# New orders of issue and new PSUM banks for a linear-attention block with a gated MLP, on one core

## The chip, the core and the metric

The kernel runs on one core of a Trainium2 chip. A core has TensorE (PE, matmuls; its weight loads are shown as PEld), VectorE (DVE), ScalarE (ACT), GpSimd (POOL) and SyncE (SP), which here issues every DMA. TensorE writes its results to PSUM, eight banks; DVE and ACT read them from there. The metric is the device time of one execution in microseconds (us), as the median of several runs.

## The reference

A block of a transformer on 2048 tokens of width 448, in bf16: linear attention with 16 heads of 28, then a gated MLP of width 1792, each behind a layernorm without weights and with a residual.

```python
h  = x + A(layernorm(x))
h2 = h + B(layernorm(h))

# A: phi(t) = where(t > 0, t + 1, exp(t)) + 1e-6
q, k, v = split(x @ wqkv)
kv  = einsum("bhsd,bhse->bhde", phi(k), v);  z = phi(k).sum(tokens)
o   = einsum("bhqd,bhde->bhqe", phi(q), kv) / (einsum("bhqd,bhd->bhq", phi(q), z) + 1e-6)
A   = o @ wo
# B
B   = (gelu(x @ w_gate) * (x @ w_up)) @ w_down
```

All of k and v must be summed over all tokens before the first q can be turned into an output, so the work falls into two halves, with the sum `kv` between them.

## The kernel before

The 2048 tokens are 16 tiles of 128. The Python code does not issue instructions as it goes. It records 942 tasks in a graph (`_Graph.add`), each with its engine, what it reads and what it writes, and numbers them in the order of recording. Two constants then say how they are issued. `ORDERS` holds five strings, one for each of PE, ACT, DVE, POOL and SP; each lists the numbers of that engine's tasks in the order in which the engine issues them. `BANKS` gives a PSUM bank to each of the 218 PSUM tiles. `place` reads both, adds to each PE task that opens a tile the dependences on whoever last wrote or read that bank, and asserts that the five orders do not wait for each other in a circle. `emit` then walks an engine's order and puts before each task the semaphore waits that it needs. Every engine works strictly in its own order: a task that waits holds up all tasks behind it on that engine. The same holds for SP's list of DMA issues.

The tasks by name (the number behind the name is the token tile, for gate/up tasks a running number v):

- Start: `dx` loads tokens, `dwkv`, `dwq`, `dwo`, `dwg`, `dwu`, `dwt`, `dwd` load weights (L342). `warm` (L401) is a burst of 36 matmuls on a tile of ones. POOL's `ones`, `ident`, `eps`, `pqones`, `mones`, `mhalf`, `mask_a` to `mask_d` and `powwarm` fill constants (L365 to L387).
- First layernorm: `ast`, `aag` (DVE statistics, L406 and L407), `anm` (POOL, the negated mean, L411), `aln`, `ars` (ACT, 1/sqrt, L416 and L418), `norm` (DVE for tiles 0 and 1, L439, else POOL, L442). Tiles 0 to 3 are transposed on TensorE (`tr`, L452 to L454) and copied by `ev`; the others by ACT's `dup` (L464) and a DMA transpose `xT` on SP (L470).
- k and v: `kva`, `kvb` (L491 to L499), 4 and 3 pairs of matmuls that use the upper and the lower half of the array's rows at once. `ek` (ACT, exp, L506), `cl` (POOL, clamp, L507), `ph` (DVE, phi(k), L508) and `evv` (ACT, copy of v, L510) empty their PSUM tiles. `acca`, `accb` (L518) add the tile's k'v to the sum in two banks.
- `kz1`, `kz2` (DVE, L534 and L536) take the finished sum out of PSUM.
- q: `qa`, `qb` for two tiles at once (L550), `eq` (ACT, L559), `cq` (POOL, L560), `pq` (DVE, L561), and a DMA transpose `qT` (L563).
- Output of the attention: `nd` (L600, L608), `rd` and `om` (DVE, L617 and L620), a transpose (`tro` and `evo` for the first pair of tiles, L631 and L634, a DMA transpose `oT` for the others, L636), `woa`, `wob` (L652), `hr` (DVE, the residual, L665), and the second layernorm: `bst`, `bag`, then for tiles 0 and 1 `bln`, `brs`, `normh` (L678), `trh` (PE, L685 and L687) and `evh` (L690), for the others POOL's `bve`, `bpw`, `bnm`, `normh` (L697), DVE's `wrap` (L699) and the DMA transpose `hT` (L700).
- MLP: `gua`, `gub` (L769, L772), 4 and 3 pairs of matmuls for each block of the width, for groups of 2, 2, 4, 4 and 4 token tiles; `ge` (ACT, gelu, L795), `hm` (DVE, product, L797). `da`, `db` (L719) are the down projection of two tiles, `down` (L733) that of the last two; `out` (DVE, L739) adds the residual and `dout` (SP, L741) stores the tile.

What decides a wait is thus: where a task stands in its engine's order, and which PSUM tile stood in its bank before. The waits are made here:

```python
for t in self.order["pe"]:
    for tile in t.allocs:
        for b in range(tile.bank, tile.bank + tile.nb):
            old = held.get(b)
            if old is not None:
                for d in [old.alloc[0]] + old.users:
                    self._dep(t, d, tile.alloc[1])
            held[b] = tile
```

Of the kernel before, what the change touches and what calls it, by code (L numbers as in the profile page):

```python
# [14 lines left out]
    "29 35 42 138 50 139 146 147 154 58 155 162 144 163 170 145 152 171 178 153 160 179 186 161 168 187 194 169 176 195 177"  # L15
    " 184 268 202 269 203 210 185 192 211 218 193 200 219 226 201 242 227 243 208 234 209 216 235 250 217 224 251 258 225 232"
    " 259 277 233 240 278 241 248 286 249 256 287 257 264 265 295 361 360 296 313 366 386 387 314 368 369 304 322 305 331 323"
    " 332 381 393 384 394 434 465 435 459 466 460 471 410 472 411 477 507 478 508 441 495 442 496 483 417 489 418 484 490 531"
    " 543 532 537 544 561 538 514 562 515 555 579 556 549 580 550 501 567 723 568 724 502 699 586 700 587 573 730 574 731 621"
    " 609 622 706 610 707 633 603 615 604 634 616 627 657 628 658 639 645 640 646 651 675 669 652 676 663 670 664 681 753 682"  # L20
    " 759 754 747 760 765 748 771 766 777 772 778 783 693 789 694 784 790 813 801 807 814 687 802 808 688 795 849 796 843 825"
    " 844 826 850 867 819 868 820 855 861 856 862 873 897 874 879 898 880 903 885 837 886 904 838 921 891 922 892 909 915 910"
    " 916 831 927 832 928 936 933 939",
    "28 32 33 39 40 47 48 51 55 56 140 65 66 143 151 68 59 78 79 71 148 159 91 81 156 167 84 92 164 175 104 172 94 180 97 183"
    " 105 188 117 118 107 191 130 196 110 123 199 131 273 120 270 207 204 133 212 215 223 220 136 228 244 231 247 239 236 255"
    " 252 263 260 279 282 288 291 300 297 318 315 306 376 309 377 378 324 379 327 333 382 336 458 469 467 463 461 473 475 481"
# [846 lines left out]
```

## Time and profile before

| what | value |
|---|---|
| median of 3 runs | 198.19 us (196.95 to 199.13) |
| span of the profiled execution | 194.1 us |
| its own time | not given apart from the span |
| instructions | 5347 |
| ACT busy | 69.6 us of the span (36%) |
| POOL busy | 48.8 us (25%) |
| HBM | 8.72 MB read, 1.84 MB written |
| granted TensorE clock | 1.000 in the mean |

The span runs from the first to the last instruction of the profiled execution; the time of a run also holds what lies before and after. In a row of a timeline the columns are the start, the duration, engine, line, operation, output and inputs, shapes, the number of instructions that were merged into the row, and in square brackets the idle time before it with what ended it. "SPq" marks the issue of a DMA on SP: its duration is that of the issue, not of the transfer. In the rows of DMA issues the last number is the time from issue to landing. The end of a matmul is modelled, so matmuls that follow each other are drawn overlapping.

### The profile page before, as it was taken

What the parts mean: (1) busy time and instruction counts of PE and PEld (TensorE: products, weight loads), DVE (VectorE), ACT (ScalarE), POOL (GpSimd) and SP (SyncE); (2) the same over time, 40 slices, a digit from 0 to 9 for tenths busy, and PEclk for the clock granted to TensorE, in tenths of its full rate; (3) what the DMA queues carried; (4) which work ended last, traced back from release to release, by engine and by line L of the source; (5) the groups of instructions that cost most, each with busy time, mean ns of one, the idle gap of its engine ahead of it and who ended that gap; (6) DMA issues with size and microseconds to landing.
All of it is one profiled execution on the core that took longest, in us unless ns stands there. A gap on an engine that the chain in (4) does not pass through costs nothing.

```text
span 194.1 us, 5347 instructions
## 1 busy us (share of the span) xinstructions
PE 188.0 (97%) x2183; PEld 108.7 (56%) x2183; DVE 114.6 (59%) x299; ACT 69.6 (36%) x201; POOL 48.8 (25%) x104
## 2 busy tenths in 40 slices
PE   7889999999999999999999999999999999999994
PEld 7336555654598798665444445444455554445563
DVE  4699453599999886668686736424251644244132
ACT  4488867443932243210025343422033432213000
POOL 2379984443605009000037630000000000000000
PEclk9999999999999999999999999999999999999999
DMA  5964645989859996523200320100403000010021
GB/s 148 288 209 94 95 89 128 284 178 195 194 114 193 223 222 178 85 56 70 47 0 3 89 69 0 27 5 0 105 3 118 2 3 0 3 47 0 3 83 59
DMA packets 41209, 18.01 MB, mean 93 GB/s; under 512 B 30177, under 2 KB 41057, under 8 KB 41185
## 3 DMA queue, kind: packets, MB, share of 16 engines
q1 hardware_dynamic: 41184, 17.67, 40.0%
q8 instruction: 17, 0.28, 0.6%
q14 instruction: 8, 0.06, 0.1%
HBM read 8.72 MB, written 1.84 MB: 54 GB/s over the span
## 4 chain that ended last, share of the span: by engine, by line
PE 66%; DMA 3%; DVE 3%; issue 0%; SPq 0%; DVEq 0%
PE ps L769 37%; PE ps L719 19%; PE ps L652 4%; DMA wgu_sb<-in_B_w_up_dram 3%; PE ps L772 3%; PE ps L733 3%; DVE pq L561 1%; PE ps L608 1%; DVE x_sb L665 1%; DVE o L620 0%; SPq L342 0%; DVE st L406 0%; DVE hh L797 0%; DVE x_sb L739 0%; DVE hnT L690 0%
## 5 line engine op out<-in xcount | busy, mean ns | idle before, releaser
L772 PE MATMUL ps<-hnT,wgu_sb 64*128 64x512 bf16 (+1 forms) x490 | 89.1, 333 | 0.2 <-DMA wgu_sb<-in_B_w_up_dram 0.2
L769 PE MATMUL ps<-hnT,wgu_sb 64*128 64x512 bf16 (+1 forms) x490 | 89.1, 333 | 0.0
L795 ACT ACTIVATE gl<-ps 128x256 bf16<-128x256 f32 x112 | 36.0, 384 | 87.4 <-PE ps L772 68.3
L797 DVE TENSOR_TENSOR hh<-ps,gl 128x256 bf16<-128x256 f32 x112 | 41.8, 414 | 39.3 <-ACT gl L795 34.9
L769 PEld LDWEIGHTS ps<-hnT,wgu_sb 64*128 64x128 bf16 x490 | 45.0, 94 | 35.0 <-DVE hh L797 2.3
L772 PEld LDWEIGHTS ps<-hnT,wgu_sb 64*128 64x128 bf16 x490 | 45.0, 94 | 0.6 <-DMA wgu_sb<-in_B_w_up_dram 0.5
L719 PE MATMUL ps<-wd_sb,hh 64*128 64x448 bf16 x392 | 38.9, 349 | 0.0
L719 PEld LDWEIGHTS ps<-wd_sb,hh 64*128 64x128 bf16 x392 | 19.1, 94 | 17.9
L406 DVE BATCH_NORM_STATS2 st<-x_sb 128x6 f32<-128x448 bf16 x32 | 19.2, 612 | 4.5 <-DMA x_sb<-in_A_x_dram 4.5
L739 DVE TENSOR_TENSOR x_sb<-ps,x_sb 128x448 bf16<-128x448 f32 (+1 forms) x17 | 9.8, 589 | 16.6 <-PE ps L719 13.3
L491 PE MATMUL ps<-wkv_sb,xnT 64*128 64x448 bf16 x64 | 14.8, 349 | 0.8 <-DMA xnT<-xn 0.4
L508 DVE SCALAR_TENSOR_TENSOR pk<-ps,tm 128x448 bf16<-128x448 f32 x16 | 9.9, 622 | 8.9 <-POOL tm L507 4.1
L492 PE MATMUL ps<-wkv_sb,xnT 64*128 64x448 bf16 x64 | 14.9, 350 | 0.0
L652 PE MATMUL ps<-wo_sb,oT 64*128 64x448 bf16 x112 | 13.4, 350 | 0.1
L550 PE MATMUL ps<-wq_sb,xnT 64*128 64x448 bf16 x112 | 12.3, 349 | 0.0
L498 PE MATMUL ps<-wkv_sb,xnT 64*128 64x448 bf16 x48 | 11.6, 352 | 0.1
L499 PE MATMUL ps<-wkv_sb,xnT 64*128 64x448 bf16 x48 | 11.6, 352 | 0.0
L665 DVE TENSOR_TENSOR x_sb<-ps,x_sb 128x448 bf16<-128x448 f32 x16 | 9.5, 616 | 2.9 <-PE ps L652 2.8
L559 ACT ACTIVATE e<-ps 128x448 bf16<-128x448 f32 x16 | 8.1, 540 | 7.9 <-PE ps L550 7.9
L560 POOL TENSOR_SCALAR tm<-e 128x448 bf16<-128x448 bf16 x16 | 8.8, 560 | 7.8 <-ACT e L559 6.9
L561 DVE SCALAR_TENSOR_TENSOR pq<-ps,tm 128x448 bf16<-128x448 f32 x16 | 9.5, 612 | 1.9 <-PE ps L492 1.2
L442 POOL TENSOR_SCALAR xn<-x_sb,nm,rs 128x448 bf16<-128x448 bf16 x14 | 10.0, 714 | 1.9 <-ACT rs L418 1.6
(70 smaller groups left out, 163.3 us busy)
## 6 DMA issues: line engine op xcount, KB each, us to landing
out_dram<-x_sb SPq DMA_DIRECT2D x15, 112.0 KB, 1.8
wd_sb<-in_B_w_down_dram SPq DMA_DIRECT2D x3, 448.0 KB, 4.4
wgu_sb<-in_B_w_up_dram SPq DMA_DIRECT2D x3, 384.0 KB, 3.8
wgu_sb<-in_B_w_gate_dram SPq DMA_DIRECT2D x3, 384.0 KB, 5.3
x_sb<-in_A_x_dram SPq DMA_DIRECT2D x2, 448.0 KB, 6.2
wo_sb<-in_A_wo_dram SPq DMA_DIRECT2D x2, 336.0 KB, 5.3
x_sb<-in_A_x_dram SPq DMA_DIRECT2D x4, 112.0 KB, 2.1
wkv_sb<-in_A_wqkv_dram SPq DMA_DIRECT2D x1, 448.0 KB, 3.6
```

The lines of the kernel that those rows point to most:

```text
L406: op("dve", lambda e: e.bn_stats(st[:, t, :], src_ap()), [b_src], [b_st[t]], nm + "st%d" % t, 0.615, key)
L491: e.matmul(ps[:, p_k.bank, 0:D], xnT[A_, k, tok], wkv_sb[A_, k, ck], start=(k == 0), stop=False, skip_group_check=True)
L492: ins = e.matmul(ps[:, p_v.bank, 0:D], xnT[B_, k, tok], wkv_sb[B_, k, cv if k < 3 else ck], start=(k == 0), stop=False, skip_group_check=True)
L498: e.matmul(ps[:, p_k.bank, 0:D], xnT[B_, k, tok], wkv_sb[B_, k, ck], start=False, stop=(k == 2), skip_group_check=True)
L499: ins = e.matmul(ps[:, p_v.bank, 0:D], xnT[A_, k, tok], wkv_sb[A_, k, cv], start=False, stop=(k == 2), skip_group_check=True)
L550: ins = e.matmul(ps[:, p_q[n].bank, 0:D], xnT[rows, k, ts[n] * 128:(ts[n] + 1) * 128], wq_sb[rows, k, :], start=(k == 0 and not second), s ...
L652: ins = e.matmul(ps[:, p_h[n].bank, 0:D], oT2[rows, so, kk, :], wo_sb[rows, kk, :], start=(k == 0 and not second and not res), stop=(secon ...
L719: ins = e.matmul(ps[:, p_d[n].bank, 0:D], hh[rows, j, u * 128:(u + 1) * 128], wd_sb[rows, j, :], start=(j == 0 and not second), stop=(j == ...
L769: e.matmul(ps[:, pa.bank, jj * N:(jj + 1) * N], wgu_sb[A_, wa + k if k < 3 else 3, jc], hnT[A_, k, c0:c0 + N], start=(k == 0 and jj == 0 a ...
L772: ins = e.matmul(ps[:, pb.bank, jj * N:(jj + 1) * N], wgu_sb[B_, wb + k if k < 3 else 3, jc], hnT[B_, k, c0:c0 + N], start=(k == 0 and jj ...
L795: G.add("act", lambda e, gi=gi, cs=cs, p_g=p_g: e.activation(gl[:, gi, cs], ps[:, p_g.bank, cs], AF.Gelu_apprx_tanh), r=[p_g], w=[b_gl[gi] ...
L797: op("dve", lambda e, dst=dst, gi=gi, cs=cs, p_u=p_u, rs_=rs_: e.tensor_tensor(dst, rs_(ps[:, p_u.bank, cs]), rs_(gl[:, gi, cs]), ALU.mult ...
```

## The change

`ORDERS` and `BANKS` are replaced; nothing else in the file differs. Each of the five strings still holds the same task numbers, so each engine issues the same instructions with the same operands except for the PSUM bank, in another order. Of the positions in the orders, 61 of 249 on PE hold the same task as before, 50 of 201 on ACT, 54 of 299 on DVE, 16 of 100 on POOL and 33 of 93 on SP. The new lists come from a search on a timing model in which transfers are late at random.

The core of the diff, the first line of each list (PE, ACT, DVE, POOL, SP) and of the banks:

```diff
@@ -12,45 +12,46 @@
 ORDERS = (
-    "29 35 42 138 50 139 146 147 154 58 155 162 144 163 170 145 152 171 178 153 160 179 186 161 168 187 194 169 176 195 177"
...
+    "29 35 42 138 139 146 50 147 58 154 144 155 162 145 163 152 153 170 160 171 161 178 186 179 187 168 194 169 176 195 177"
...
-    "28 32 33 39 40 47 48 51 55 56 140 65 66 143 151 68 59 78 79 71 148 159 91 81 156 167 84 92 164 175 104 172 94 180 97 183"
...
+    "28 32 39 33 40 47 48 140 55 56 143 65 66 51 148 68 59 78 71 79 151 156 159 81 91 164 84 167 92 172 175 94 104 117 105"
...
-    "30 31 37 18 38 34 44 41 45 20 36 43 52 53 60 62 61 63 75 76 73 74 86 88 89 142 87 127 150 101 99 158 100 102 114 166 112"
...
+    "30 37 44 31 18 38 34 41 36 20 45 43 52 53 60 62 61 63 142 73 75 74 76 88 86 150 87 89 101 158 114 99 100 102 115 166"
...
-    "10 12 11 19 46 49 54 57 64 67 70 141 77 80 149 83 157 90 93 165 96 173 103 116 181 106 189 109 122 197 119 129 274 23"
...
+    "19 23 10 11 12 46 21 24 49 22 54 141 57 64 67 70 149 77 80 157 90 83 165 93 96 103 173 106 181 116 189 109 119 197 122"
...
-    "0 1 2 3 4 5 6 7 8 9 16 13 17 69 72 82 85 15 14 95 98 108 111 124 121 342 134 346 137 345 343 276 344 340 355 285 341 353"
...
+    "0 1 2 3 4 5 6 7 8 9 16 15 17 69 72 82 85 13 14 95 98 352 108 121 111 124 276 134 137 354 346 345 341 349 342 285 343"
...
 BANKS = (
-    "0 1 0 0 2 6 1 2 3 4 0 5 2 4 5 1 4 3 1 0 3 2 1 0 3 2 5 0 1 2 5 3 0 4 1 2 3 4 4 5 5 2 1 4 5 3 6 0 1 2 5 4 3 7 7 6 7 7 3 2"
...
+    "3 6 1 6 4 6 5 3 0 2 5 3 4 1 2 0 5 1 3 4 0 2 5 3 2 0 1 3 4 3 0 5 1 2 3 0 4 1 4 1 2 5 0 3 5 1 1 6 3 2 5 0 3 7 4 6 4 5 4"
```

The same in names, at the places that matter below (before, then after):

```
PE    warm tr0 tr1 kva0 tr2 kvb0 kva1 kvb1 kva2 tr3 kvb2 kva3 acca0 kvb3 kva4 accb0 acca1 kvb4 kva5 accb1 acca2 kvb5 kva6 ...
      warm tr0 tr1 kva0 kvb0 kva1 tr2 kvb1 tr3 kva2 acca0 kvb2 kva3 accb0 kvb3 acca1 accb1 kva4 acca2 kvb4 accb2 kva5 kva6 kvb5 ...
PE    ... qa4 accb13 acca14 qb4 accb14 acca15 accb15 qa6 nd1 nd0 qb6 qa10 tro nda2 ndb2 qb10 woa0 wob0 qa8 qa12 qb8 qa14 qb12 qb14
          trh0 woa2 trh1 wob2 nda6 gua1 ndb6 gua0 ...
      ... qa4 accb12 acca13 qb4 accb13 acca14 accb14 acca15 accb15 qa6 qb6 nd1 nd0 qa10 nda2 qb10 tro ndb2 qa8 woa0 wob0 qb8 qa14 qa12
          qb14 qb12 woa2 wob2 trh0 trh1 nda6 gua1 ndb6 gua0 ...
PE    ... woa6 gua6 wob6 gub6 gua4 woa4 gua5 wob4 gub4 gub5 gua7 gua9 ...
      ... woa6 ndb8 wob6 gua6 gua4 gub6 gub4 woa4 gua5 wob4 gub5 gua8 gua10 ...
PE    ... da10 gub49 gub52 db10 ... da8 da12 db8 db12 down15_0 down14_0 down15_224
      ... da10 gua55 gua53 gua54 gub53 gub54 gub55 db10 da8 da12 db8 db12 down14_0 down15_0 down15_224
ACT   tbl aln0 ars0 aln1 ars1 aln2 ars2 ev2 aln3 ars3 ek0 aln4 ars4 evv0 evv1 dup4 ev3 aln6 ars6 dup5 ek1 ...
      tbl aln0 aln1 ars0 ars1 aln2 ars2 ek0 aln3 ars3 evv0 aln4 ars4 ev2 ek1 dup4 ev3 aln6 dup5 ars6 evv1 ...
DVE   ast0 aag0 ast1 pkones aag1 norm0 ast2 norm1 aag2 ...
      ast0 ast1 ast2 aag0 pkones aag1 norm0 norm1 ev0 v1ones aag2 ...
DVE   ... ph15 pq2 pq3 kz2 kz1 pq4 rd1 rd0 om1 om0 pq5 pq7 evo ... normh0 pq8 pq9 normh1 pq12 pq13 evh1 hr2 hr3 ...
      ... pq3 pq2 ph15 kz1 pq4 kz2 pq5 rd1 rd0 om1 om0 pq7 pq6 evo ... normh0 pq11 normh1 pq12 hr3 evh1 hr2 ...
POOL  ones eps ident pqones anm2 norm2 anm3 norm3 anm4 norm4 norm5 cl0 ...
      pqones mones ones ident eps anm2 mhalf mask_a norm2 powwarm anm3 cl0 norm3 anm4 norm4 norm5 cl1 ...
SP    ... dx6 dx8 dwq0 dx12 xT4 xT5 xT6 xT7 dwq_t1 dwq_t0 xT8 xT9 xT10 xT11 xT13 xT12 dwo_u xT14 dwt0_0 xT15 ...
      ... dx6 dx8 dwq_t1 dx12 xT4 xT5 xT6 xT7 dwq0 dwq_t0 xT8 xT9 dwt0_1 xT10 xT12 xT11 xT13 qT0 xT14 xT15 dwg3 ...
SP    ... oT4 dwd1 hT3 hT2 oT8 dwd0 qT10 ...
      ... oT4 qT10 hT3 hT2 oT8 dwd2 dwd0 dwd1 qT14 dwd3 ...
SP    ... hT12 dout4 dout6 dout5 dout0 dout7 dout10 dout11 dout8 dout9 dout13 dout15_0 dout14 dout12 dout15_224
      ... hT12 dout2 dout1 dout8 dout5 dout11 dout3 dout4 dout12 dout7 dout9 dout13 dout6 dout10 dout15_0 dout14 dout15_224
```

63 rows, old and new, of tables (BANKS, ORDERS) are left out of this document.

## The prediction

> **What bounds the kernel now.** I read the first page, then busy time by stretch of time, then the timelines of single engines and of SyncE's DMA queue. Only one execution is profiled, and its own time is given as the span alone, 194.1 us; the median of the runs, 198.19, lies 4.1 us above it. I make the sums against the span and add those 4.1 us at the end.
>
> ```profile
> span 194.1 us, 5347 instructions
> PE 188.0 (97%) x2183; PEld 108.7 (56%) x2183; DVE 114.6 (59%) x299; ACT 69.6 (36%) x201; POOL 48.8 (25%) x104
> ```
>
> TensorE is busy nearly from end to end, and its instructions are the same after the change. What an order can win is therefore the time in which TensorE waits. Where that is:
>
> ```profile
> 0.00:14.63 14.63, 12.25 (x117) 7.18 (x118) 9.66 (x29) 8.43 (x25) 6.65 (x20) 1.00 0.73 214
> 14.63:39.06 24.43, 23.86 (x331) 14.34 (x332) 13.92 (x30) 17.36 (x48) 17.39 (x37) 1.00 0.65 141
> 39.06:52.73 13.67, 13.22 (x152) 6.70 (x153) 13.49 (x32) 7.36 (x18) 7.12 (x13) 1.00 0.91 185
> 52.73:64.38 11.65, 11.44 (x210) 10.15 (x211) 11.24 (x32) 3.76 (x11) 2.58 (x5) 1.00 0.78 167
> 64.38:191.35 126.97, 126.97 (x1375) 70.32 (x1376) 65.86 (x179) 32.70 (x102) 15.06 (x30) 1.00 0.24 53
> 191.35:194.10 2.75, 0.26 (x3) 0.01 (x1) 0.39 (x1) 0.00 (x0) 0.00 (x0) 1.00 0.32 104
> ```
>
> The columns are the stretch and its length, then busy time of PE, PEld, DVE, ACT, POOL, the granted clock, DMA share and GB/s. From 64.38 to the last matmul TensorE never rests: nothing is to be won there, only lost. Before 14.63 it waits for the first tokens. Between 14.63 and 64.38 it waits little by this view, but a matmul is drawn 0.35 us long while the next starts 0.19 later, so each wait hides up to 0.16:
>
> ```profile
> 14.63 0.35 PE L491 MATMUL ps<-wkv_sb,xnT 64*128 64x448 bf16 x1
> ...
> 14.82 0.35 PE L491 MATMUL ps<-wkv_sb,xnT 64*128 64x448 bf16 x1
> ...
> 37.81 0.37 PE L518 MATMUL ps<-v,pk 64*113 64x113 bf16 x8
> 38.04 0.74 PE L550 MATMUL ps<-wq_sb,xnT 64*128 64x448 bf16 x6
> 38.62 0.75 PE L518 MATMUL ps<-v,pk 64*113 64x113 bf16 x12
> 39.21 0.92 PE L550 MATMUL ps<-wq_sb,xnT 64*128 64x448 bf16 x8
> 40.22 0.57 PE L600 MATMUL ps<-kvz,pqT 113*128 113x116 bf16 x8
> 40.73 1.52 PE L550 MATMUL ps<-wq_sb,xnT 64*128 64x448 bf16 x14
> ```
>
> So I count work by issue: 0.19 us for a pair of half-row matmuls of 448 columns, 0.23 us for two acc tasks (37.81 to 38.04). From 14.63 (kva4) to 39.06 (accb15) the order has twelve tiles' kva and kvb of 7 pairs together, the q tasks of three pairs of tiles, 7 each, and 30 acc: 84 x 0.19 + 21 x 0.19 + 15 x 0.23 = 23.4 us, in 24.4. From 39.06 to 52.73 (the first gate/up task, gua1) it has 35 pairs of q and 14 of wo, 9.3 us; five nd at 0.25 (two from 40.22 to 40.73) and 17 transposes at about 0.06 bring 2.3 more: 11.6 in 13.7. In that stretch DVE is full (13.49 of 13.67), so DVE's chain sets when the gate/up matmuls can start. About 3.1 us stand open in these two stretches.
>
> **The change part by part.** No instruction is added or removed; each step below is a move.
>
> *Start.* DVE now does ast0, ast1, ast2 before aag0, and POOL does pqones and mones before ones, and mhalf, mask_a and powwarm around norm2.
>
> ```profile
> 0.78 0.20 POOL L365 MEMSET ones_bf<- 128x128 bf16 x1 [0.29 <-POOLq L858]
> ...
> 1.30 0.42 POOL L375 MEMSET pq<- 128x384 bf16 x1
> ```
> ```profile
> 2.82 0.63 DVE L406 BATCH_NORM_STATS2 st<-x_sb 128x6 f32<-128x448 bf16 x1 [2.82 <-DMA x_sb<-in_A_x_dram]
> 3.48 0.18 DVE L407 BATCH_NORM_AGGREGATE mv<-st 128x2 f32<-128x6 f32 x1
> 3.58 0.59 DVE L406 BATCH_NORM_STATS2 st<-x_sb 128x6 f32<-128x448 bf16 x1
> ...
> 4.31 0.37 DVE L439 TENSOR_SCALAR xn<-x_sb,mv,rs 128x448 bf16<-128x448 bf16 x1
> ```
> ```profile
> 1.04 3.77 PE L401 MATMUL ps<-ones_bf 128*128 128x128 bf16 x36 [1.04 <-POOL eps_t L368]
> 4.74 0.34 PE L452 MATMUL ps<-ident,xn 128*128 128x128 bf16 x3
> ```
>
> aag0 slips by two statistics, 3.48 to about 4.55, and norm0 and tr0 with it: tr0 at about 5.8 instead of 4.74. The warm-up burst starts 0.4 us later. I cost both at nothing, because another chain is later: kva4 waits for the first DMA transpose.
>
> ```profile
> 6.54 0.51 SPq L342 DMA_DIRECT2D wq_sb<-in_A_wqkv_dram  x1
> 7.08 0.49 SPq L342 DMA_DIRECT2D x_sb<-in_A_x_dram  x1
> 12.01 5.31 SPq L470 DMA_TRANSPOSE xnT<-xn  x4
> 17.37 1.22 SPq L342 DMA_DIRECT2D wq_sb<-in_A_wqkv_dram  x2
> 18.69 8.87 SPq L470 DMA_TRANSPOSE xnT<-xn  x6
> ```
> ```profile
> xnT<-xn SPq DMA_TRANSPOSE x12, 2.5
> ...
> wgu_sb<-in_B_w_up_dram SPq DMA_DIRECT2D x3, 384.0 KB, 3.8
> ...
> wq_sb<-in_A_wqkv_dram SPq DMA_DIRECT2D x1, 336.0 KB, 6.1
> ```
>
> xT4 is issued at 12.01 and lands 2.5 later, 14.5; kva4 follows at 14.63. Its own chain (x4 and x5 landed, aag4, ars4, norm4, dup4) does not go through tr0, and TensorE's work ahead of kva4 fits: it now also holds accb0, acca1 and accb1, 0.3 us that used to come after. If that cover is gone, because ACT now does ek0, ev2 and ek1 ahead of dup4, the bound is the whole slip of 1.1 us. Value taken: 0, since ek1 needs kvb1, which ends near 10.3 (5.8, three groups of transposes at some 0.4, 14 pairs, and the drawn 0.35 of the last), and ACT is at ars4 until 10.8 as before:
>
> ```profile
> 10.62 0.20 ACT L418 ACTIVATE rs<-ln 128x2 f32<-128x2 f32 x1
> ```
>
> *Stage 14.63 to nd1.* kva6 now follows kva5 at once: TensorE reaches it after 14.63 + 2 x 0.76 + 0.57 + 0.2 = 16.9, but xT6 is third in a row of 1.33 us issues, 12.01 + 2.66 + 2.5 = 17.2: a new wait of 0.35. The large wq load moves from 6.54 to behind xT7, 17.4, with dwq_t0, xT8 and everything later queued behind it on SP; dx12 gets its place. At 3.8 us (the nearest row: a load of like size with transposes ahead of it in the queue) it lands at 21.2; qa0 is due at about 21.1, and the small piece lands a little after: 0.3 us. Bounds: 0 (under 3.7 us) and 2.4 (at 6.1). Sum: 14.63 + 84 x 0.19 + 21 x 0.19 + 27 acc x 0.115 + 0.35 + 0.3 = 38.3 for accb15, 0.75 earlier than now. evv15 now comes after ek15 on ACT, so ph15 is not later than that.
>
> Then the DVE order:
>
> ```profile
> 39.41 0.22 DVE L536 TENSOR_TENSOR kvz<-ps,mask 113x16 bf16<-113x16 f32 x1
> 39.50 0.62 DVE L534 TENSOR_TENSOR kvz<-ps,mask 113x448 bf16<-113x448 f32 x1
> 40.04 0.62 DVE L561 SCALAR_TENSOR_TENSOR pq<-ps,tm 128x448 bf16<-128x448 f32 x1
> ...
> 52.21 0.41 DVE L690 COPY hnT<-ps 128x512 bf16<-128x512 bf16 x1
> ```
>
> nd1 needs kz1 and kz2, now with pq4 between them: 0.54 (39.50 to 40.04) that used to follow. nd1 comes at 40.22 - 0.75 + 0.54 = 40.0. qb6 runs before it, 0.57 us of work that covers the wait. From nd1 to evh1 the chain on DVE is the same but for one full-width operation: pq11, pq12 and hr3 stand between normh0 and evh1 where pq8, pq9, pq12, pq13 stood. One is worth 0.54. gua1, which followed evh1 at 52.73, comes at about 52.7 - 0.2 - 0.5 = 52.0. New here: nda6 takes hr3's PSUM bank side, so it and gua1 behind it wait for hr3; evh1 is behind hr3 anyway, so nothing more.
>
> *From gua1.* The bank moves and the other swaps put gua4 behind hr6, and gua8 and gua10 behind hT3 and hT2, which go behind qT10 on SP. A transpose there costs 1.25 us of SP:
>
> ```profile
> 62.38 2.50 SPq L700 DMA_TRANSPOSE hnT<-hn  x2
> ```
>
> Walking DVE forward from evh1 at its 0.33 to 0.54 us steps, hr6 ends within 0.2 us of TensorE's arrival and hT2 lands between 0.5 us before and 0.6 us after it. I take 0.1; bounds 0 and 0.7. hT5 before gua15 is as close. After that everything has room of a microsecond or more, and TensorE is full as it is now.
>
> *End.*
>
> ```profile
> 190.96 1.51 SPq L741 DMA_DIRECT2D out_dram<-x_sb  x3
> 191.72 0.39 DVE L739 TENSOR_TENSOR x_sb<-ps,x_sb 128x224 bf16<-128x224 f32 x1 [0.79 <-PE ps L733]
> ```
>
> Eleven outputs now stand behind dout8, which db8 releases some 7 us before the end. Fourteen issues at 0.45 us (three in 1.51, waits included) are 6.3 us: dout14_0 is gone 0.3 us before dout15_224 is ready. Zero; at 0.6 an issue it would be 0.7.
>
> **Sum**: -0.7 at gua1, +0.1 behind it, 0 at the end: -0.6, span 193.5 us, and with 4.1 around it 197.6 us.
>
> **The rivals.**
>
> *All waits go.* The new order looks ahead further, and nearly all of the 3.1 us found above is won: 198.19 - 3 = 195.2. For it: TensorE waits nowhere for its own work. Against it: DVE is full from 39 to 64, with the same instructions, and gua1 hangs on it.
>
> *Nothing arrives.* What is won at gua1 is given back at gua8, where hT2 (after wrap2, normh2 and qT10's issue) is the last to come: 198.2. For it: the four engines in that chain and a transpose of 2.5 us; against: woa4, gua5, wob4 and gub5 stand between gua4 and gua8, some 3 us of cover.
>
> *Slower: wq late.* If the load takes 6.1 us again from its new place, qa0 starts at 23.5 instead of 21.1. All that follows up to gua1 is paced by TensorE's q and kv results, so the 2.1 us beyond my 0.3 stay: 197.6 + 2.1 = 199.7. It is slower than now from a landing of 4.6 us on. For it: the same load's own row, and 18.69 to 27.56, six transposes of 1.25 in 8.87, shows the queue can stall there. Against: at 6.54 six large loads stood ahead of it; at 17.4 only transposes do.
>
> *Cold clock.* The 36 warm-up matmuls take 0.10 us each, and the three transposes after them, of the same 128 columns, 0.34 together although each is drawn to its own end: the clock rises during the burst. Now the burst begins 0.4 later, and 0.7 us of idling follows it. Should the rise be missed, the first kv matmuls, 2.6 us, take twice as long, kvb1, ek1 and dup4 slip, and kva4 by up to 1.2: 198.8. [...]
>
> **How the numbers follow.** Forecast 0.42, all waits go 0.14, nothing arrives 0.22, wq late 0.17, cold clock 0.05. Predicted 197.6 us; the forecast's own range, from its bounds (gua1 up to 1.2 earlier by DVE alone, waits behind it up to 0.7), is 196.4 to 198.3. To hold 8 in 10 the range reaches from just below the first rival to wq late: 194.9 to 199.8. One per cent, about 2 us, is what a measurement of this kernel can tell from no change (its three runs spread 1.1%). Faster by more: 0.14 and some of the forecast's low side, 0.24. Slower by more, over 200.2: wq later still, the clock, and what I have not seen in the zero-slack places, 0.13. Within 1%: 0.63.
>
> **What would show it.** Right: tr0 near 5.8 yet kva4 near 14.6; a short wait at kva6 for xT6 and at qa0 for wq; accb15 near 38.3; kz2 after pq4; gua1 near 52.0; no wait of TensorE after 70. Wrong: kva4 later than 15 (the start is not covered); qa0 after 22.5 (wq); gua1 before 51 (DVE was not the bound); a new wait above 0.5 us at gua4, gua8 or gua15; a second stretch of slow matmuls after 5 us.

## The result and the profile after

The kernel after takes 199.95 us in the median of 8 runs (198.36 to 202.86), the kernel before 197.80 beside it (8 runs, 196.39 to 199.13). The ratio is 1.0104, with a 95% interval of 1.0059 to 1.0149: about 2 us slower, where 0.6 us faster was forecast and 199.8 was the end of the range. The profiled execution of after took 198.36 us at a span of 196.6, so 1.8 us lie around a span. By that the profiled execution of before (span 194.1) was itself a quick one, near 195.9, and the 4.1 us that the prediction added to it were 1.8 us around the span and 2.3 us of spread between runs. Medians and ranges below are of all executions, ratios leave out those that ran slowed as a whole, and where the profiled execution was one of these its times are not used.

The head of the page of after; the columns are busy time, share of the span and instructions:

```profile
span 196.6 us, 5351 instructions
...
PE 189.4 (96%) x2183; PEld 115.8 (59%) x2183; DVE 114.2 (58%) x299; ACT 69.4 (35%) x201; POOL 48.9 (25%) x104
```

The same stretches as in the prediction, in the kernel after (columns as there: PE, PEld, DVE, ACT, POOL, clock, DMA share, GB/s):

```profile
0.00:14.63 14.63, 12.20 (x121) 7.92 (x122) 9.73 (x29) 8.05 (x25) 7.85 (x25) 1.00 0.68 194
14.63:39.06 24.43, 24.03 (x320) 14.69 (x316) 14.36 (x29) 17.14 (x48) 16.82 (x34) 1.00 0.69 137
39.06:52.73 13.67, 13.25 (x151) 6.48 (x151) 12.39 (x29) 6.29 (x16) 6.07 (x11) 1.00 1.00 195
52.73:64.38 11.65, 11.46 (x220) 9.99 (x220) 11.18 (x33) 4.57 (x11) 3.11 (x6) 1.00 0.78 180
64.38:191.35 126.97, 125.66 (x1355) 74.20 (x1350) 65.26 (x179) 33.38 (x104) 15.04 (x30) 1.00 0.22 48
191.35:196.60 5.25, 2.76 (x29) 2.51 (x27) 1.31 (x3) 0.00 (x0) 0.00 (x0) 1.00 0.52 171
```

Two things differ from before. Ahead of 64.38 no stretch is much fuller or emptier, except that DVE is no longer full between 39.06 and 52.73 (12.39 of 13.67). And from 64.38 on, where TensorE of before never rested, 1.31 us are open. The timeline of TensorE shows where; this is the last matmul pair of `gub5` and the first of `gua8`:

```profile
67.85 0.27 PE L770 MATMUL ps<-hnT,wgu_sb 64*128 64x256 bf16 x1
67.87 0.27 PE L773 MATMUL ps<-hnT,wgu_sb 64*128 64x256 bf16 x1
69.24 0.27 PE L770 MATMUL ps<-hnT,wgu_sb 64*128 64x256 bf16 x1 [1.10 <-DVE mv L408]
```

Pairs follow at 0.11 us, so `gua8` was due at 67.96 and waits 1.28 us. The view names a DVE statistic as the releaser, but that was done at 68.77, 0.47 us before `gua8` started; it is a DMA, as SP's queue shows next (`hT2` lands at 69.14). The name of a releaser has to be held against its own end.

Split at this point, the difference of the two profiled spans closes. TensorE is through with the work ahead of the second pair of token tiles at 67.96, in before at 67.89: +0.07. Then come +1.28 of wait, and then the same set of tasks up to the last matmul:

```profile
69.24:193.85 124.61, 124.39 (x1321) 73.69 (x1322) 61.32 (x170) 31.41 (x98) 15.04 (x30) 1.00 0.21 49
```

In before this set runs from `gua7` to the last matmul:

```profile
67.89:191.35 123.46, 123.46 (x1325) 67.34 (x1321) 63.08 (x174) 32.25 (x101) 15.06 (x30) 1.00 0.21 48
```

That is +1.15. The tail is 2.75 us in both. 0.07 + 1.28 + 1.15 = 2.5, the 196.6 against 194.1.

**Why hT2 is late.** SP's queue in the kernel after, from the issue of `qT10` on:

```profile
62.38 1.31 SPq L564 DMA_TRANSPOSE pqT<-pq  x1
63.79 2.53 SPq L701 DMA_TRANSPOSE hnT<-hn  x2
67.08 1.43 SPq L637 DMA_TRANSPOSE oT<-o  x1
```

`hT3` is issued at 63.79 and `hT2` behind it at 65.11, 1.4 us later than in before (62.38 and 63.67). The chain that leads there begins with `bst2`. On DVE the statistics of tiles 3 and 2 in after, then POOL's whole chain (`bve2`, `bnm2`, `bpw2`, and `normh3` and `normh2` in one row):

```profile
56.28 0.62 DVE L407 BATCH_NORM_STATS2 st<-x_sb 128x6 f32<-128x448 bf16 x1
60.27 0.62 DVE L407 BATCH_NORM_STATS2 st<-x_sb 128x6 f32<-128x448 bf16 x1
```
```profile
61.45 0.22 POOL L424 TENSOR_SCALAR ln<-mv 128x2 f32<-128x2 f32 x1 [7.42 <-DVE mv L408]
...
62.76 1.43 POOL L698 TENSOR_SCALAR hn<-x_sb,nm,rs 128x448 bf16<-128x448 bf16 x2
```

And the same in before, where `bst2` came first and `bst3` at 56.99:

```profile
53.61 0.62 DVE L406 BATCH_NORM_STATS2 st<-x_sb 128x6 f32<-128x448 bf16 x1
```
```profile
59.87 0.23 POOL L423 TENSOR_SCALAR ln<-mv 128x2 f32<-128x2 f32 x1 [7.18 <-DVE mv L407]
```

The change put `bst2` behind `rd4`, `rd5`, `om4` and `om5`, so POOL starts 1.58 us later. That alone would not do it: 2.44 us after its issue, as transposes of its kind land (their median is 2.4 us in before and 2.5 in after), `hT2` would be there at 67.55, 0.4 ahead of TensorE. But its flight is slow. The two `hT` transposes issued there land after (shortest, median, longest):

```profile
DMA to landing us min/median/max: 2.4/3.2/4.0
```

`hT3` took 2.4, `hT2` 4.0. What the 16 DMA engines did from 67.10 to 68.40, in 40 slices of 0.03 us (busy share of all 16 in tenths, rounded down, then the queue that matters):

```profile
DMA  9000000000000000000000000000010000024799
...
q8 instruction: 1, 0.02, 4.5%
```

The row looks empty for 0.9 us, but it isn't: one packet of 16 KB, on a queue called instruction, runs from 67.11 on. It takes 4.5% of the time of 16 engines in this window of 1.30 us, which is 0.93 us of one engine, and one busy engine of 16 is drawn as 0. A transpose of this kind is 544 packets (so many move for `hT2` in the first try below, from 68.10 to 69.42). In after the queue of the transposes moved, from 66.25 to 67.25 and then from 67.25 to 68.17:

```profile
q1 hardware_dynamic: 540, 0.13, 65.1%
```
```profile
q1 hardware_dynamic: 4, 0.00, 1.1%
```

So nearly all of `hT2` went as always. Its last four packets started only from 68.03 on, when that packet was over (67.11 + 0.93 = 68.04), and the landing came 1.0 us behind them. In the runs with the front and with the end of before, below, the last two packets start within 0.02 us of the end of that packet as well, at 71.17 and 67.87. The page of after counts 17 such packets in the whole span ("q8 instruction: 17, 0.28, 0.6%"). TensorE has 2183 matmuls and as many weight loads; 4366 instructions by 17 are 257 for each packet. By this count, which is an estimate, they are taken here for the fetches of TensorE's program; with 54 of TensorE's instructions taken out there is none from 66.0 to 69.5, and one comes at 71.64 (below).

**The late waits.** Behind `gua8` no single wait is long. The timeline of TensorE shows the 0.22 us step of the pairs break at `gua48`:

```profile
159.16 0.38 PE L770 MATMUL ps<-hnT,wgu_sb 64*128 64x512 bf16 x1
159.51 0.37 PE L773 MATMUL ps<-hnT,wgu_sb 64*128 64x512 bf16 x1
```

and ACT at that time is at the two halves of `ge41`:

```profile
158.71 0.66 ACT L796 ACTIVATE gl<-ps 128x256 bf16<-128x256 f32 x2
```

They read bank 7, which the new assignment gives to the second tile of `gua48`; it is free at 159.37, 0.2 us after TensorE came. By the orders and banks of the file, `gua27`, `gua30`, `gua44`, `gua48`, `gua50` and `gua51` each wait 0.13 to 0.35 us for a bank that a `ge` or `hm` task just then leaves. These six make 1.14 of the 1.15 us. (The expectations below call `gua44`, which waits 0.35 for `hm42` at 152.40, by its neighbour's name `gua46`, and count `db12` as a seventh with 0.28; but the step of 0.28 us behind `db12` stands in before too, so it is no loss.)

### The profile page after: what moved, and what is told of

It is laid out like the page before. It is cut to its first block, busy times and chain, and to the rows that moved or that the text cites. A ratio compares the mean times of both kernels' runs of the same rounds, so it can differ in the third digit from the quotient of the medians.

```text
span 196.6 us, 5351 instructions
## 1 busy us (share of the span) xinstructions
PE 189.4 (96%) x2183; PEld 115.8 (59%) x2183; DVE 114.2 (58%) x299; ACT 69.4 (35%) x201; POOL 48.9 (25%) x104
## 4 chain that ended last, share of the span: by engine, by line
PE 78%; DVE 7%; issue 3%; POOL 2%; DMA 2%; ACT 1%; DVEq 0%
PE ps L773 23%; PE ps L720 18%; PE ps L770 15%; PE ps L551 6%; PE ps L653 4%; PE ps L734 3%; PE ps L492 2%; DVE st L407 2%; DMA xnT<-xn 2%; PE ps L609 1%; DVE hh L798 1%; PE ps L519 1%; PE ps L499 1%; PE ps L500 1%; DVE o L621 1%
## 5 line engine op out<-in xcount | busy, mean ns | idle before, releaser
L720 PE MATMUL ps<-wd_sb,hh 64*128 64x448 bf16 x392 | 39.9, 349 | 0.0
L720 PEld LDWEIGHTS ps<-wd_sb,hh 64*128 64x128 bf16 x392 | 20.4, 94 | 16.6
L492 PE MATMUL ps<-wkv_sb,xnT 64*128 64x448 bf16 x64 | 14.6, 348 | 0.6 <-DVE st L407 0.2
L493 PE MATMUL ps<-wkv_sb,xnT 64*128 64x448 bf16 x64 | 14.7, 350 | 0.0
L412 POOL TENSOR_SCALAR nm<-mv 128x2 f32<-128x2 f32 (+1 forms) x15 | 3.3, 225 | 36.6 <-DVE mv L408 29.8
L499 PE MATMUL ps<-wkv_sb,xnT 64*128 64x448 bf16 x48 | 11.4, 351 | 0.1
L500 PE MATMUL ps<-wkv_sb,xnT 64*128 64x448 bf16 x48 | 11.4, 351 | 0.0
L507 ACT ACTIVATE e<-ps 128x448 bf16<-128x448 f32 x16 | 8.7, 542 | 5.4 <-PE ps L500 5.3
```

Of the source, the lines that this page charges most:

```text
L492: e.matmul(ps[:, p_k.bank, 0:D], xnT[A_, k, tok], wkv_sb[A_, k, ck], start=(k == 0), stop=False, skip_group_check=True)
L493: ins = e.matmul(ps[:, p_v.bank, 0:D], xnT[B_, k, tok], wkv_sb[B_, k, cv if k < 3 else ck], start=(k == 0), stop=False, skip_group_check=True)
L499: e.matmul(ps[:, p_k.bank, 0:D], xnT[B_, k, tok], wkv_sb[B_, k, ck], start=False, stop=(k == 2), skip_group_check=True)
L500: ins = e.matmul(ps[:, p_v.bank, 0:D], xnT[A_, k, tok], wkv_sb[A_, k, cv], start=False, stop=(k == 2), skip_group_check=True)
L720: ins = e.matmul(ps[:, p_d[n].bank, 0:D], hh[rows, j, u * 128:(u + 1) * 128], wd_sb[rows, j, :], start=(j == 0 and not second), stop=(j == ...
```

## The experiments

Every kernel was timed against before in 5 rounds. Where an order is taken from both kernels, the PSUM banks go with it.

**The front of before.**

```diff
-ORDERS, BANKS: after
+ORDERS, BANKS: before up to accb13, after from accb14 on
```

> The order of before up to accb13 (all five engines, with its PSUM banks), the order of after from accb14 on. Theory 1 (the change's loss is made behind gua1: 1.3 us at gua8, where hT2 is late, and about 1 us of short bank waits behind gua14): gua1 comes within 0.4 us of the 53.34 of after, gua8 still waits 1 us or more, the ratio to before stays at 1.008 to 1.012. Rival (the start of the change costs: tr0 1.25 us later, kz2 behind pq4): gua1 comes at 52.6 or earlier and everything behind it as much earlier, ratio 1.003 to 1.007. Third (the fetch of TensorE's instructions that falls on hT2's flight is chance): gua8 may lose its wait here only because the fetch falls elsewhere, with hT2 landing 2.5 us after its issue instead of 4.0.

200.99 us, ratio 1.0143 (1.0088 to 1.0199). `gua8` waits 1.27 us, `hT2` flies 4.15 us with a fetch in it, and five of the six late waits stand where they stood with their lengths (`gua44` waits 0.06). `gua1` comes at 56.64, not within 0.4 us of 53.34: the seam adds a wait of 1.66 us at `qa6`, and `xT15` flies 4.60 us with a fetch in it (1.99 us at `kva15`), which is why the ratio lies above the forecast one. So the loss is not made by the front of the change; what the front is worth this run can't say.

**The end of before.**

```diff
-ORDERS, BANKS: after
+ORDERS, BANKS: after up to gub5, before from gua7 on
```

> The order of after up to gub6 and hT2 (ahead of gua8), the order of before from gua7 on. Theory 1: the last third of the loss goes (gua46, gua27 and the other short waits, about 1.0 us), and the wait for hT2 goes too or shrinks, since gua7 is put ahead of it or hides part of it: TensorE ends 1.0 to 2.3 us earlier than in after, ratio 0.999 to 1.005. Rival (what is lost is lost ahead of gua8, and the short waits behind it lie within what repeated runs differ by): ratio 1.008 to 1.011.

197.73 us, ratio 1.0014 (0.9982 to 1.0045): theory 1. The stretch from `gua7` to the last matmul is as in before:

```profile
69.25:192.81 123.56, 123.56 (x1321) 67.85 (x1322) 61.14 (x170) 31.38 (x98) 14.93 (x30) 1.00 0.21 50
```

1.05 us of the 1.15 are back. The wait ahead of it is not: `hT2` lands 4.0 us after its issue here too, and `gua7` waits 1.32.

**hT3 and hT2 ahead of qT10.**

```diff
-" 340 294 353 344 392 303 347 312 348 355 350 440 351 416 321 409 406 513 358 356 357 339 359 585 330 430 457 729 454"
+" 340 294 353 344 392 303 347 312 348 355 350 440 351 416 409 406 321 513 358 356 357 339 359 585 330 430 457 729 454"
```

> The kernel after with hT3 and hT2 issued ahead of qT10 on SP, nothing else. Theory 1a (the place in the queue is what makes hT2 late): hT2 is issued at its wrap2 at about 64.5 instead of 65.11, lands within 2.6 us, gua8 follows gub7 without a wait above 0.2 us; 1.3 us earlier at gua8, ratio 1.003 to 1.005. Rival 1b (its slow flight of 4.0 us is what makes it late, from the 16 KB fetch of TensorE's instructions at 67.1): the issue moves by 0.6, the flight is again 3.5 us or more if the fetch falls in it, and gua8 still waits 0.5 to 1.3 us; ratio 1.006 to 1.010. Rival 1c: the wait goes at gua8 and comes back at the later short waits; ratio 1.008 or more with gua8 free.

199.04 us, ratio 1.0076 (1.0036 to 1.0116). 1a falls: `hT2` is issued at 65.33, no earlier than before the move, since `hT3` starts at 64.05, when its last `wrap3` is done (64.02), and not when SP is free. It flies 4.31 us, with the fetch at 67.62 in it, and `gua8` waits 1.51. The interval holds 1b and 1c alike and some of 1a; the ratio itself tells little. The wait that stays tells that the place behind `qT10` is not the cause.

**The fetches moved, first try.**

```diff
-for _ in range(WARM):
-    ins = e.matmul(ps[:, p_warm.bank, 0:128], ones_bf[:], ones_bf[:], start=True, stop=True)
+for _ in range(9):
+    ins = e.matmul(ps[:, p_warm.bank, 0:512], ones_bf[:, 0:128], ones_bf[:], start=True, stop=True)
```

> The kernel after with its warm-up as 9 matmuls of 512 columns in place of 36 of 128 (as many columns, 54 PE instructions fewer, counting the weight loads), so that every fetch of PE's instructions falls 54 instructions later; orders and banks as in after. Theory 1b (hT2's flight of 4.0 us comes from the fetch at 67.11): the fetch near 67 moves to about 68.4, hT2 lands 2.4 to 2.7 us after its issue, gua8 waits less than 0.2 us, and the time falls by 1.0 to 1.3 us, ratio 1.003 to 1.006; where another transpose is hit, its own flight grows by 1 us or more. Rival 1a (the queue, not the fetch): hT2's flight stays at 3.5 us or more with no fetch in it, ratio 1.008 to 1.012.

199.06 us, ratio 1.0091 (1.0061 to 1.0121). The edit also makes `ones_bf` 512 columns wide. The flight behaves as 1b says: the fetch now comes at 71.64 (68.4 was expected; that a fetch comes at a fixed count of instructions is thus not shown), and from the issue of `hT2` at 66.97 to its landing there is no packet of that queue; the only gap is the one between the two transposes:

```profile
DMA  9999999953100000000269999999963100000000
...
q1 hardware_dynamic: 1034, 0.25, 49.8%
```
```profile
DMA to landing us min/median/max: 2.4/2.4/2.4
```

`gua8` does not wait at all. The ratio, though, misses the 1.003 to 1.006 of 1b and lies where the rival had it, as the second half of 1b's expectation allowed without a price: other transposes are hit, `xT5` (3.93 us), `xT12` (5.25) and `oT8` (4.78), and TensorE waits 0.84 at `kva5`, 1.42 at `kva12` and 0.98 at `woa8`.

**The end of after behind before.**

```diff
-ORDERS, BANKS: before
+ORDERS, BANKS: before up to gub5, after from gua8 on
```

> The order of before up to its gub6, the order and PSUM banks of after from gua8 on: the converse of the run with the end of before. Theory (the order of after behind gua8 costs 1.3 to 1.6 us by itself, in the waits of gua27, gua30, gua46, gua48, gua50, gua51 and db12 of 0.13 to 0.35 us each, where a PSUM bank is handed on less than 0.3 us ahead of its next user): the same waits stand at the same tasks, the time is 1.2 to 1.7 us above before, ratio 1.006 to 1.009, though everything ahead of gua8 is as in before. Rival (the waits come only because TensorE in after arrives shifted by its wait for hT2): no such waits, ratio 0.998 to 1.003.

200.37 us, ratio 1.0147 (1.0095 to 1.0199): slower than expected. The late waits stand at the same tasks with the same lengths (0.13, 0.13, 0.35, 0.15, 0.19, 0.19), though all came 2.6 us later than in after: they belong to the order and the banks. The rest is 1.9 us at the seam, around `gua8`, and 1.64 at `kva4`: `xT4` flew 4.0 us, with a fetch at 12.97. The front is that of before, whose first fetch came at 12.04 (and at 11.66 in the run with the front of before). So where the first fetch falls changes from one execution to the next.

**The front of after before the rest of before.**

```diff
-ORDERS, BANKS: before
+ORDERS, BANKS: after up to qa6, before from there on
```

> The order and banks of after up to qa6 (the stage of the first tokens and of k, v, q), the order of before from there on. Forecast on record: accb15 0.75 us earlier. Theory (the front of the change wins nothing: tr0 1.25 us later is covered, but xT6, xT10 and xT11 are waited for one by one instead): accb15 at 39.3 to 40.3 against 39.06 in before, ratio 0.999 to 1.004. Rival (the front is worth its forecast and only the rest spoils it): accb15 at 38.6 or earlier, ratio 0.995 to 0.998.

201.68 us, ratio 1.0213 (1.0163 to 1.0262): a miss for both. The seam is again at `qa6`, where the run with the front of before lost 1.66 us. What the front is worth this run does not show.

**The fetches moved less, two kernels.** In the kernel with the end of before, and in before itself:

```diff
-for _ in range(WARM):
+for _ in range(22):
-    ins = e.matmul(ps[:, p_warm.bank, 0:128], ones_bf[:], ones_bf[:], start=True, stop=True)
+    ins = e.matmul(ps[:, p_warm.bank, 0:208], ones_bf[:, 0:128], ones_bf[:, 0:208], start=True, stop=True)
```

> The kernel with the order of after up to gub6 and of before behind it (197.73 us, ratio 1.0014, with a wait of 1.32 us at gua7 for hT2, whose flight of 4.01 us holds a fetch of PE's instructions at 66.9), with the warm-up as 22 matmuls of 208 columns in place of 36 of 128 (28 PE instructions fewer). Theory (the fetch in hT2's flight costs the 1.3 us): the fetch moves behind hT2's landing, gua7 waits less than 0.3 us; if no other transpose that TensorE waits for is hit instead, the ratio is 0.993 to 0.997, faster than before and after. Rival (the 1.3 us come back somewhere else, since each fetch hits some transpose): ratio 0.999 to 1.004. If the fetch stays in hT2's flight, nothing changes, 1.001.

> The kernel before with the same warm-up of 22 matmuls of 208 columns, as a control: what moving the fetches does where the orders are those of before. There the fetch at 67.30 falls just behind hT2's landing (67.15) and that at 22.34 lengthens xT10 to 4.14 us (kva10 waits 0.28). Theory: the fetches go 0.5 to 1.5 us later, hT2 is not hit, xT10 may be spared and xT11 or xT12 be hit instead; ratio 0.996 to 1.003. Rival (the warm-up of fewer and longer matmuls itself changes the start): tr0, kva0 or kva4 move by over 0.5 us.

198.93 us, ratio 1.0091 (1.0052 to 1.0131), and 198.38 us, ratio 1.004 (1.0004 to 1.0076): the first above every value that was expected, the second just above the theory's. `ones_bf` is 256 columns wide in both. In the first, `hT2` lands 2.44 us after its issue, as the theory says, but the rival is right about the time: the first fetch, at 13.52, now falls into `xT4`, which flies 4.2 us, and `kva4` waits 1.51. Nor is `gua7` free, as the theory had it: it still waits 0.78, for its bank 6, which `hr5` reads until 70.33. In before with the same warm-up `xT4` is hit in the same way. TensorE around `kva4`, in the kernel before with 22 matmuls of warm-up:

```profile
14.39 0.35 PE L498 MATMUL ps<-wkv_sb,xnT 64*128 64x448 bf16 x1
16.73 0.35 PE L491 MATMUL ps<-wkv_sb,xnT 64*128 64x448 bf16 x1 [1.99 <-DMA xnT<-xn]
```

The landing of `xT4`, issued at 12.2, and the DMA engines from 14.20 to 15.50:

```profile
DMA to landing us min/median/max: 4.4/4.4/4.4
```
```profile
DMA  2229000000000000000246999899999999999929
...
q8 instruction: 1, 0.02, 5.4%
```

The 0.5 us of zeros are not the sign of the fetch: the first try above shows the same pause between two transposes with no fetch near. The sign is the landing, 4.4 us after the issue, with the fetch's packet of 1.1 us (5.4% of 16 engines in 1.30 us) in the flight from 14.31 on. In this kernel `hT3` flies 5.7 us as well, with the fetch at 67.8, and `gua7` waits 2.20. So before becomes a little slower (the interval just excludes no change) by an edit that takes instructions away and moves nothing; the warm-up's own length accounts for less, `tr0` moves by 0.20 us and `kva0` by 0.16.

**The chain to hT2 started earlier.**

```diff
 DVE
-... hm1_0 rd4 rd5 om4 om5 bst2 hm2_0 bag3 bag2 hm2_1 hm3_0 rd9 hr6 rd8 hr7 wrap3 hm3_1 wrap2
+... hm1_0 bst2 bag3 bag2 rd4 rd5 om4 om5 hm2_0 hm2_1 hm3_0 rd9 wrap3 hr6 wrap2 rd8 hr7 hm3_1
 SP
-... oT4 qT10 hT3 hT2
+... oT4 hT3 hT2 qT10
```

> The kernel after with eight moves: on DVE bst2, bag3 and bag2 ahead of rd4 (in after they stand behind om5, bst2 at 60.27; in before bst2 is at 53.61), wrap3 ahead of hr6 and wrap2 ahead of rd8; on SP hT3 and hT2 ahead of qT10. Theory (what makes gua8 wait is the place of bst2 on DVE, which starts POOL's chain bve2, bpw2, bnm2, normh3, normh2 at 61.45, and the fetch only lengthens it): bve2 starts near 59.9, hT2 is issued near 63.8 and lands near 66.4, ahead of the fetch at 67; gua8 follows gub5 without a wait above 0.2 us, 1.0 to 1.3 us earlier; the waits behind gua14 stay, 1.4 us; ratio 1.002 to 1.006. Rival (oT4, now behind om4 and om5 0.9 later, makes woa4 wait instead): gua8 at the same time as in after, ratio 1.008 or more.

198.12 us, ratio 1.0049 (1.0015 to 1.0082), where after in the same rounds has 1.0125: 0.0076, 1.5 us back (0.4 to 2.6 by the two intervals). That `gua8` no longer waits is read from the run with both repairs, below.

**The same moves with the end of before.**

```diff
-ORDERS, BANKS: after up to gub5, before from gua7 on
+the same, with the moves of the run above
```

> The same moves in the kernel that has the order of after up to gub5 and of before from gua7 on. Theory: both losses go, the wait of 1.3 us ahead of gua7 and the 1.4 us of the late bank waits; against the 1.0014 of that kernel without the moves 0.8 to 1.3 us less, ratio 0.994 to 0.998. Rival (each kernel has its hits of the fetch somewhere, and a wait taken away there leaves others to decide): ratio 0.999 to 1.004.

197.64 us, ratio 1.0063 (1.0026 to 1.0101): missed. `hT2` lands at 68.05, 1.5 us ahead of TensorE, but `gua7` starts at 70.46 instead of 69.61, since its bank 6 is still read by `hr5` until 70.40. That wait of the seam lay hidden behind `hT2` in the kernel without the moves.

The profiled execution (198.62 us, where seven of the twelve lie between 197.34 and 197.70) shows a second loss. TensorE in `kva0`:

```profile
7.62 0.58 PE L493 MATMUL ps<-wkv_sb,xnT 64*128 64x448 bf16 x1
7.99 0.58 PE L492 MATMUL ps<-wkv_sb,xnT 64*128 64x448 bf16 x1
```

The pairs are 0.37 us apart, twice the 0.19 of the other executions with this front, and stay so until 10.8. `kva4` comes at 16.50, against 15.18 in the kernel without the moves, with the same order up to there. This is what the prediction's cold clock would look like. The column of the granted clock in the views by stretch has 1.00 for this time, so it is the distance of the matmuls that shows it; that the clock is the cause is not shown.

**Other banks.**

```diff
-BANKS of after
+BANKS of after ahead of gua15; from gua15 on each tile takes the bank that has been free longest (93 tiles)
```

> The kernel after with its orders, but from gua15 on each PSUM tile takes the bank that the profile of after shows free for the longest time (93 tiles change their bank). Theory (the late waits are banks handed on too soon): the waits of gua27, gua30, gua46 and gua51 go (0.80 us); gua48 and gua50 keep theirs (0.15 and 0.19), since no bank is free earlier at their place in TensorE's order, and so does db12 (0.28, no bank); 0.6 to 0.9 us less from gua14 to the end than in after. Rival (the waits are in the orders of DVE and ACT, whatever the bank): waits of 1.2 us or more in sum remain.

198.36 us, ratio 1.0071 (1.0037 to 1.0105), 0.0054 or 1.1 us better than after in the same rounds. The stretch from `gua8` to the last matmul, with every order as in after:

```profile
70.17:193.76 123.59, 123.59 (x1321) 69.51 (x1322) 60.84 (x168) 31.42 (x98) 15.08 (x30) 1.00 0.22 50
```

1.02 us of the 1.15 are back; 0.14 at `gua50` stays, as expected, and `gua48` lost its wait too, which was not expected. The two intervals leave 0 to 2.1 us for the 1.1; it is the stretch that shows the gain. `hT2` is hit here as well (3.98 us), and `gua8` waits 1.82.

**After once more.**

> The kernel after once more, on the same chip as the three others, to show which of its waits are there each time. Theory: gua8 waits 1.0 to 1.5 us for hT2 and the seven late waits stand at the same tasks with the same lengths to 0.05 us; ratio 1.007 to 1.013. Rival (chance of one execution): the wait of gua8 is below 0.5 us or the late waits stand elsewhere.

199.44 us, ratio 1.0125 (1.0083 to 1.0167): the loss is the same as the first time. Which waits stand where in a second execution of after itself this run does not show. The run with `hT3` and `hT2` ahead of `qT10`, which is after but for three places on SP, has the wait at `gua8` and all six late ones with their lengths.

**Both repairs together.**

```diff
-ORDERS, BANKS: after
+ORDERS: after with the moves on DVE and SP; BANKS: those of the run with other banks
```

> The kernel after with both repairs: the eight moves that start the norm of tiles 2 and 3 earlier (bst2, bag3, bag2, wrap3, wrap2, hT3, hT2) and the banks of the run that reassigned them from gua15 on. Theory (the loss of after is these two places and no third): hT2 lands before TensorE is through with gub5, gua8 waits less than 0.3 us, the late waits come to 0.3 to 0.5 us; against the 1.0125 of after the 1.5 us of the one and the 1.1 us of the other add up: ratio 0.997 to 1.002. Rival (a third loss further ahead, at the start or in the k, v, q stage): ratio 1.003 or more although both waits are gone.

196.59 us in 12 runs (196.06 to 198.36), beside 197.51 of before; ratio 0.997 (0.9934 to 1.0007). The loss of after is these two places; no third shows in the time. TensorE from 64.38 to `gua8`, and from there to the last matmul:

```profile
64.38:67.91 3.53, 3.53 (x58) 3.20 (x56) 3.09 (x8) 1.31 (x4) 0.00 (x0) 1.00 0.89 80
67.91:191.59 123.68, 123.68 (x1326) 69.53 (x1321) 62.76 (x173) 32.08 (x100) 15.09 (x30) 1.00 0.22 52
```

`gua8` comes at 67.91 without a wait. POOL's chain and SP's queue:

```profile
59.63 0.22 POOL L424 TENSOR_SCALAR ln<-mv 128x2 f32<-128x2 f32 x1 [5.63 <-DVE mv L408]
```
```profile
62.53 2.54 SPq L701 DMA_TRANSPOSE hnT<-hn  x2
```

`hT2` is issued at 63.85 and lands 2.44 us later, at 66.28, just ahead of the fetch at 66.6.

**The front of after with the end of before, its seam mended.**

```diff
-BANKS of the run with the same moves and the end of before
+from gua7 on each tile takes the bank that has been free longest (114 tiles)
```

> The kernel with the order of after up to gub5, the eight moves, and the order of before from gua7 on, with the PSUM banks from gua7 on given anew by the longest free one (in the profile of that kernel gua7 waited 0.85 us for bank 6, which hr5 still read, although hT2 had landed 1.5 us ahead). Theory: gua7 follows gub5 within 0.2 us, no late waits; 0.8 us less than the 1.0063 of that kernel: ratio 1.000 to 1.004; below 1.000 only if the front of after is worth something. Rival (the front wins its forecast 0.7 us): ratio 0.995 to 0.999.

196.75 us, ratio 0.9981 (0.995 to 1.0011). By the ratios it is 1.6 us faster than the same kernel with the seam's bank, twice what was expected. The value falls to the rival's side (a front that is worth something), but the interval holds both cases. That `gua7` follows without a wait is not shown here, only the time. Neither this kernel nor the one above can be told from before; that the front of after wins a little, at most 0.7% by the lower ends, stays open.

## Why the prediction was wrong

**Start: nearly right.** `tr0` came at 5.99 (5.8 forecast) and its slip of 1.25 us was covered. `kva4` came at 15.11, past the mark of 15: 0.3 us of acc work now stands ahead of it, and `xT4` took 1.60 us to issue and landed at 14.89. No second stretch of slow matmuls shows in this execution, the kv pairs are 0.19 us apart from 7.08 on: the cold clock did not make this loss. But the rival is not out. Of the eight profiled executions with this front whose times are used (two with another warm-up), one has the slow stretch (the same moves with the end of before), and `kva4` comes 1.3 us later there; the prediction had up to 1.2. In before the warm-up matmuls start 0.107 us apart up to 4.32 and 0.056 from 4.43 on; in after they start 0.107 apart to the end of the burst, the last at 5.14, and the transposes from 5.99 on 0.06. What sets the moment at which the step falls no run shows.

**The stage to accb15: wrong by 1.3 us.** Of the two new waits one was near (`kva6` 0.23 for 0.35 forecast); at `qa0` (21.57 for 21.4) there is none, since TensorE came 0.2 us behind the landing of the small piece of wq (21.40). The rival with wq late is out, the load took 3.2 us from its new place. But the sum let all other waits of the old order go and put none in their place. They came back at other tasks. TensorE at `kva10` and `kva11`, then from `accb13` to `nd1`:

```profile
25.66 0.35 PE L500 MATMUL ps<-wkv_sb,xnT 64*128 64x448 bf16 x1
26.10 0.35 PE L492 MATMUL ps<-wkv_sb,xnT 64*128 64x448 bf16 x1
...
28.43 0.27 PE L519 MATMUL ps<-v,pk 64*113 64x113 bf16 x4
28.84 0.35 PE L492 MATMUL ps<-wkv_sb,xnT 64*128 64x448 bf16 x1
```
```profile
38.66 1.23 PE L519 MATMUL ps<-v,pk 64*113 64x113 bf16 x20
39.73 1.73 PE L551 MATMUL ps<-wq_sb,xnT 64*128 64x448 bf16 x14
41.39 0.38 PE L601 MATMUL ps<-kvz,pqT 113*128 113x116 bf16 x4
```

0.25 us are lost at `kva10` (0.44 between pairs where 0.19 is the step) and 0.3 at `kva11`, each for its transpose, and 20 acc matmuls take 1.07 where 0.6 was counted. `accb15` came at 39.58 for 38.3.

**nd1 and gua1: right in length, wrong in place.** `kz2` does stand behind `pq4` (0.54 us), and from `nd1` at 41.39 to `gua1` at 53.34 are 11.95 us, 12.0 by the forecast. So the -0.7 at `gua1` failed by what came in from the stage ahead: it was +0.6. `gua1` still follows `evh1` (done at 53.23), but DVE was full in this stretch before and had 1.3 us open after, so its length is no longer DVE's alone.

**From gua1: the step that failed.** `hT2` was to land between 0.5 us before TensorE's arrival and 0.6 after it, at a cost of 0.1 (bounds 0 and 0.7); the wait was 1.28. The walk along DVE was good: with the usual 2.44 us of flight `hT2` lands 0.4 before. The term that was mis-sized is the flight, 4.03 us. It was 3.98 to 4.31 in all five profiled kernels with this part of after in which a fetch began 1.0 to 2.3 us after the issue, 2.44 in the three, with the moves or another warm-up, where none fell into the flight, and 2.44 in one where the fetch came 0.1 us ahead of the landing. That a delay of 1.6 us could decide here goes back to `bst2`: the slack of 0.4 is what was left after POOL's chain had been started 1.58 us later, and putting `bst2` and what follows from it back ahead brought 1.5 us. The rival "nothing arrives" named this place and priced it as a gain given back; there was no gain to give. Against the forecast span of 193.5 us the miss is 3.1: TensorE came to `gua8` 0.8 us later than forecast, the wait there was 1.2 above the 0.1, and 1.15 came behind it.

**"After that everything has room of a microsecond or more": the other step that failed.** It looked at transposes alone. The banks are part of the change, and at six tasks the bank was released 0.1 to 0.5 us after TensorE had come for it; 1.14 us were lost there, and other banks brought 1.02 back.

**End: right.** The stores are issued in one train:

```profile
186.72 8.26 SPq L742 DMA_DIRECT2D out_dram<-x_sb  x14
```

It ends 0.4 us past the sum that brings the last half tile (194.61), whose own store is the last of them: nothing is waited for, and the tail is 2.75 us in both.

**The chances.** 0.13 for slower by more than 1% held what "I have not seen in the zero-slack places". TensorE without a pause in the last 127 us meant that an order could only lose there, and a new assignment of every bank was a way to lose that had no rival of its own.

## What to carry to other kernels

Where one engine is full, walk each new order not only for what the full engine waits for, but back through the whole chain of a late transfer to the first small task in it: here one 0.6 us statistic was put behind four other tasks, and starting its chain earlier brought some 1.5 us. A PSUM bank that goes to a new tile just when its last reader should be done becomes a wait as soon as that reader is a little late: here six waits of 0.13 to 0.35 us, 1.14 in sum, of which 1.02 came back with the bank that had been free longest. And leave DMA transposes on which TensorE hangs some 1.9 us of slack, an estimate from the flights of `hT2`: 4.31 us at most with a fetch in them, 2.44 without.

## What the runs showed of the hardware

What is called a fetch of TensorE's program here is a packet of 16 KB on the queue called instruction, 17 in before and 17 in after, one for about 257 of TensorE's instructions; it took 0.88 to 1.60 us. The DMA transposes `hT2` and `xT4`, in flight with one, landed 4.0 us and more after their issue instead of 2.4 (`hT2`: 3.98 to 4.31 in five kernels with the fetch 1.0 to 2.3 us after the issue, 2.44 in three without and in one where it came 0.1 us ahead of the landing; `xT4` 4.0 to 4.4 in three kernels, 2.5 to 2.9 where the fetch came within 0.3 us of the issue); `xT10` of after, with a fetch 1.1 us after its issue, took 3.7. Most of `hT2` moves as always: in after and in the runs with the front and with the end of before, all but two to four of its 544 packets do, and the first of these last ones starts within 0.02 us of the end of the fetch. A fetch is not the only thing that slows a transpose: in before, where the load `dwd1` stands just ahead of them in SP's queue, `hT3` and `hT2` took 4.29 and 3.48 us with no fetch in flight. With two changes of the warm-up alone the fetches came elsewhere (at 71.64 for 67.11 with 9 matmuls, at 14.31 for 12.04 with 22), and with them the slow flights. TensorE waited 0.8 to 2.2 us for a transpose that a fetch had met (`kva5` of the first try 0.84, `gua8` of after 1.28, `kva4` of before with 22 matmuls 2.15). Why a few packets start only when the fetch is over, and why the landing comes 1.0 to 1.3 us behind the last of them (0.3 where no fetch is near), the runs do not show.

The first fetch came at 12.04 in one execution and at 12.97 in another with the same front, once harmless and once at a price of 1.6 us. That may be a part of the spread of before (195.65 to 202.11 in 32 runs), as may the slow stretch of matmuls at the start, which cost 1.3 us in one execution; neither was tested.
